# One ring for all bulk transfers, and one semaphore for all stores, in a layer-scale kernel

## The chip, the cores and the metric

The kernel runs on one core of a Trainium2 chip. The metric is device time in microseconds (us) of one execution. All runs named here were fast, at a granted clock of 1.0 (the share of its full clock that TensorE was given). A profile's span is some 1.3 us shorter than the time of the same execution (119.8 us against 121.17 us before the change), so spans are compared with spans and times with times.

Three words recur. A ring is the queue of transfers that one issuing engine (SP or ACT) fills. A packet is the piece of a transfer, here 32 KB, of which the trace has one record on a DMA engine. A transfer has landed when its semaphore says that all its data have arrived.

## The reference

```python
B, S, D = 1024, 16, 512            # x, y: bf16 (B, S, D); gamma: bf16 (D,)
def reference(x, y, gamma):
    return x + gamma * y
```

Two inputs of 16.8 MB are read and one output of 16.8 MB is written: 50.33 MB in all.

## The kernel before

Each of the 128 partitions gets 128 rows of 512 elements, in four pieces of 32 rows. A piece is 4 MB (4096 KB) of x, of y or of the output, and each partition's share of it is 32 KB in one run of memory. All of y has its place on the chip; x has two buffers that are used in turn, so the third x load must wait for the first addition, and the fourth for the second.

The x loads go through the SP ring, the y loads through the ACT ring, and the stores are shared between the two. VectorE multiplies y by gamma in place, then adds x in place.

```python
    # SP ring
    first.append(load(nc.sync, xs[0], xv[:, piece(0), :], s_x[0]))
    first.append(load(nc.sync, xs[1], xv[:, piece(1), :], s_x[1]))
    _take(s_sp, 1, nc.sync)                                   # first addition done
    load(nc.sync, xs[0], xv[:, piece(2), :], s_x[2])
    _take(s_sp, 1, nc.sync)                                   # second addition done
    load(nc.sync, xs[1], xv[:, piece(3), :], s_x[3])
    nc.sync.dma_start(out=ov[:, piece(0), :], in_=y_sb[:, piece(0), :]).then_inc(s_out_sp, 16)
    _take(s_sp, 1, nc.sync)
    nc.sync.dma_start(out=ov[:, piece(2), :], in_=y_sb[:, piece(2), :]).then_inc(s_out_sp, 16)
    # ACT ring (gamma was issued first)
    for c in range(n):
        i = load(nc.scalar, y_sb[:, piece(c), :], yv[:, piece(c), :], s_y[c])
        ...
    _take(s_act, 1, nc.scalar)
    nc.scalar.dma_start(out=ov[:, piece(1), :], in_=y_sb[:, piece(1), :]).then_inc(s_out_act, 16)
    _take(s_act, 1, nc.scalar)
    nc.scalar.dma_start(out=ov[:, piece(3), :], in_=y_sb[:, piece(3), :]).then_inc(s_out_act, 16)
    # VectorE, for each piece c
    ... tensor_tensor(out=yt, in0=yt, in1=gamma_sb broadcast, op=MULT)      # L98
    ... tensor_tensor(out=yt, in0=xs[c % 2], in1=yt, op=ADD)                # L104
    ...
    _take(s_out_sp, 32, nc.sync)                              # the end
    _take(s_out_act, 32, nc.sync)
```

Of the kernel before, what the change touches and what calls it, by code (L numbers as in the profile page):

```python
# [3 lines left out]

PIECE = 32
MULT, ADD = mybir.AluOpType.mult, mybir.AluOpType.add


def _take(sem, n, eng):


    return eng.wait_ge(sem, n).then_inc(sem, -n)  # L12


def kernel(
    tc: tile.TileContext,
    x: bass.AP,
    y: bass.AP,
    gamma: bass.AP,
    out: bass.AP,  # L20
):




    nc = tc.nc
    P = nc.NUM_PARTITIONS
    tc.close()
    tc.compile()  # L29

    xf = x.flatten_outer_dims()
    yf = y.flatten_outer_dims()
    of = out.flatten_outer_dims()
    N, D = xf.shape
    rows = N // P
    n = rows // PIECE
    dt = xf.dtype
    xv = xf.rearrange("(p n) d -> p n d", p=P)
    yv = yf.rearrange("(p n) d -> p n d", p=P)
    ov = of.rearrange("(p n) d -> p n d", p=P)  # L40

    gamma_row = nc.alloc_sbuf_tensor("gamma_row", [1, D], dt).ap()
    ones_row = nc.alloc_sbuf_tensor("ones_row", [1, P], dt).ap()
    gamma_sb = nc.alloc_sbuf_tensor("gamma_sb", [P, D], dt).ap()
    y_sb = nc.alloc_sbuf_tensor("y_sb", [P, rows, D], dt).ap()
    xs = [nc.alloc_sbuf_tensor(f"x{i}", [P, PIECE, D], dt).ap() for i in range(2)]
    gamma_ps = nc.alloc_psum_tensor("gamma_ps", [P, D], mybir.dt.float32).ap()

    sem = nc.alloc_semaphore
    s_gamma, s_ones, s_ps, s_dve = sem("s_gamma"), sem("s_ones"), sem("s_ps"), sem("s_dve")  # L50
    s_x = [sem(f"s_x{c}") for c in range(n)]
    s_y = [sem(f"s_y{c}") for c in range(n)]
    s_sp, s_act = sem("s_sp"), sem("s_act")
    s_out_sp, s_out_act = sem("s_out_sp"), sem("s_out_act")

    def piece(c):
        return slice(c * PIECE, (c + 1) * PIECE)

    first = []

    def load(eng, dst, src, s):
        return eng.dma_start(out=dst, in_=src).then_inc(s, 16)


    first.append(load(nc.scalar, gamma_row, gamma.unsqueeze(0), s_gamma))
    nc.vector.memset(ones_row, 1.0).then_inc(s_ones, 1)  # L66
    _take(s_ones, 1, nc.tensor)
    _take(s_gamma, 16, nc.tensor)
    nc.tensor.matmul(gamma_ps, ones_row, gamma_row, start=True, stop=True).then_inc(s_ps, 1)  # L69
    _take(s_ps, 1, nc.vector)  # L70
    nc.vector.tensor_copy(out=gamma_sb, in_=gamma_ps).then_inc(s_dve, 1)  # L71
    _take(s_dve, 1, nc.vector)


    first.append(load(nc.sync, xs[0], xv[:, piece(0), :], s_x[0]))
    first.append(load(nc.sync, xs[1], xv[:, piece(1), :], s_x[1]))
    _take(s_sp, 1, nc.sync)
    load(nc.sync, xs[0], xv[:, piece(2), :], s_x[2])
    _take(s_sp, 1, nc.sync)
    load(nc.sync, xs[1], xv[:, piece(3), :], s_x[3])  # L80
    nc.sync.dma_start(out=ov[:, piece(0), :], in_=y_sb[:, piece(0), :]).then_inc(s_out_sp, 16)
    _take(s_sp, 1, nc.sync)
    nc.sync.dma_start(out=ov[:, piece(2), :], in_=y_sb[:, piece(2), :]).then_inc(s_out_sp, 16)


    for c in range(n):
        i = load(nc.scalar, y_sb[:, piece(c), :], yv[:, piece(c), :], s_y[c])
        if c < 2:
            first.append(i)
    _take(s_act, 1, nc.scalar)  # L90
    nc.scalar.dma_start(out=ov[:, piece(1), :], in_=y_sb[:, piece(1), :]).then_inc(s_out_act, 16)
    _take(s_act, 1, nc.scalar)
    nc.scalar.dma_start(out=ov[:, piece(3), :], in_=y_sb[:, piece(3), :]).then_inc(s_out_act, 16)

    for c in range(n):
        yt = y_sb[:, piece(c), :]
        _take(s_y[c], 16, nc.vector)
        nc.vector.tensor_tensor(  # L98
            out=yt, in0=yt, in1=gamma_sb[:, None, :].to_broadcast([P, PIECE, D]), op=MULT
        ).then_inc(s_dve, 1)  # L100
        _take(s_x[c], 16, nc.vector)
        _take(s_dve, 1, nc.vector)

        i = nc.vector.tensor_tensor(out=yt, in0=xs[c % 2], in1=yt, op=ADD)  # L104
        if c == 0:
            i.then_inc(s_sp, 1)
        elif c == 1:
            i.then_inc(s_dve, 1)
            _take(s_dve, 1, nc.vector)
            nc.vector.sem_inc(s_sp, 1)  # L110
            nc.vector.sem_inc(s_act, 1)
        else:
            i.then_inc(s_sp if c == 2 else s_act, 1)

    _take(s_out_sp, 32, nc.sync)
    _take(s_out_act, 32, nc.sync)

    main = nc.main_func.blocks[0].instructions
    names = {i.ins.name for i in first}
    for b in nc.main_func.blocks[1:]:  # L120
        for i in [i for i in b.instructions if i.name in names]:
            b.instructions.remove(i)
    for k, i in enumerate(first):
        main.insert(1 + k, i.ins)


# [1 line left out]
_INS = ['x', 'y', 'gamma']  # L128
_OUTS = [((1024, 16, 512), 'bfloat16')]


# [23 lines left out]
```

## Time and profile before

| | before |
|---|---|
| time, median of the 3 runs | 121.11 us (121.06 to 121.39) |
| span of the profile | 119.8 us |
| VectorE busy | 70.3 us, done at 95.0 us |
| both DMA queues, share of the 16 engines' span | 49.9% + 48.7% = 98.6% |
| mean rate | 420 GB/s |

These lines are from the profile page of the kernel before. The rows with 40 digits or numbers are 40 slices of 3.0 us each; the lines q1 (the SP ring) and q10 (the ACT ring) give packets, MB, and the share of the 16 engines' span; the last two lines are the chain of work that ended last.

```profile
span 119.8 us, 90 instructions
PE 0.6 (0%) x1; PEld 0.1 (0%) x1; DVE 70.3 (59%) x10; POOL 0.2 (0%) x4
...
DMA  8999998989898989898999989999999999989994
GB/s 274 427 427 448 405 470 361 514 350 525 350 525 350 525 350 525 350 492 383 437 437 427 448 372 405 405 394 481 394 481 394 448 427 438 437 383 470 405 470 197
...
q1 hardware_dynamic: 864, 25.17, 49.9%
q10 hardware_dynamic: 866, 25.17, 48.7%
...
DVE 7%; issue 0%
DVE y_sb L104 7%
```

There is no idle slice in the DMA row, and the two shares add up to 98.6%. The chain at the bottom is of no use here: it follows instructions and stops at the last addition, since what came after it was only transfers. The alternation of 350 and 525 GB/s is not a real swing. A packet counts in the slice in which it starts, and a slice holds two or three packets of each engine.

These lines are from the timeline of the kernel before: start, duration, engine (SPq and ACTq are the issuing of DMAs), source line, operation.

```profile
24.24 8.69 DVE L98 TENSOR_TENSOR y_sb<-y_sb,gamma_sb 128x16384 bf16<-128x16384 bf16 x1 [18.12 <-DVEq L12]
...
59.56 0.35 ACTq L91 DMA_DIRECT2D out_dram<-y_sb  x1
...
86.31 8.69 DVE L104 TENSOR_TENSOR y_sb<-x,y_sb 128x16384 bf16<-128x16384 bf16 x1
95.11 0.35 ACTq L93 DMA_DIRECT2D out_dram<-y_sb  x1
```

VectorE stands still for 18 us at the start and ends 25 us before the span does. Neither costs anything as long as the DMA engines always have something to move.

The trace has a record of each DMA packet, and these give the sum of the span. All bulk data move in 1536 packets of 32 KB, 96 on each engine, and nearly every one takes 1.213 us. Over 16 engines that is 16 x 32768 bytes / 1.213 us = 432 GB/s. The Trainium skill ("DMA: Bandwidth & Descriptors", section "Where 436 GB/s comes from") puts the ceiling at 435.2 GB/s; this trace agrees within 1%. So 96 x 1.213 = 116.4 us of the span are fixed by the bytes, and only some 3 us are left to win or lose.

### The profile page before, as it was taken

What the parts mean: (1) busy time and instruction counts of PE and PEld (TensorE: products, weight loads), DVE (VectorE), ACT (ScalarE), POOL (GpSimd) and SP (SyncE); (2) the same over time, 40 slices, a digit from 0 to 9 for tenths busy, and PEclk for the clock granted to TensorE, in tenths of its full rate; (3) what the DMA queues carried; (4) which work ended last, traced back from release to release, by engine and by line L of the source; (5) the groups of instructions that cost most, each with busy time, mean ns of one, the idle gap of its engine ahead of it and who ended that gap; (6) DMA issues with size and microseconds to landing.
All of it is one profiled execution on the core that took longest, in us unless ns stands there. A gap on an engine that the chain in (4) does not pass through costs nothing. (4 is left out here: it accounts for less than half of the span.)

```text
span 119.8 us, 90 instructions
## 1 busy us (share of the span) xinstructions
PE 0.6 (0%) x1; PEld 0.1 (0%) x1; DVE 70.3 (59%) x10; POOL 0.2 (0%) x4
## 2 busy tenths in 40 slices
PE   0100000000000000000000000000000000000000
PEld 0000000000000000000000000000000000000000
DVE  0100000099999999999899999999999700000000
POOL 0000000000000000000000000000000000000000
DMA  8999998989898989898999989999999999989994
GB/s 274 427 427 448 405 470 361 514 350 525 350 525 350 525 350 525 350 492 383 437 437 427 448 372 405 405 394 481 394 481 394 448 427 438 437 383 470 405 470 197
DMA packets 1730, 50.33 MB, mean 420 GB/s; under 512 B 193, under 2 KB 194, under 8 KB 194
## 3 DMA queue, kind: packets, MB, share of 16 engines
q1 hardware_dynamic: 864, 25.17, 49.9%
q10 hardware_dynamic: 866, 25.17, 48.7%
HBM read 33.56 MB, written 16.78 MB: 420 GB/s over the span
## 5 line engine op out<-in xcount | busy, mean ns | idle before, releaser
L98 DVE TENSOR_TENSOR y_sb<-y_sb,gamma_sb 128x16384 bf16<-128x16384 bf16 x4 | 34.8, 8690 | 18.9 <-DVEq L12 18.9
L104 DVE TENSOR_TENSOR y_sb<-x,y_sb 128x16384 bf16<-128x16384 bf16 x4 | 34.8, 8692 | 0.6
L71 DVE CAST gamma_sb<-gamma_ps 128x512 bf16<-128x512 f32 x1 | 0.7, 692 | 2.6 <-DVEq L12 2.6
L66 DVE MEMSET ones_row<- 1x128 bf16 x1 | 0.2, 165 | 2.7 <-PEq L29 2.7
L69 PE MATMUL gamma_ps<-gamma_row,ones_row 1*128 1x512 bf16 x1 | 0.6, 581 | 4.7 <-PEq L12 4.7
L69 PEld LDWEIGHTS gamma_ps<-gamma_row,ones_row 1*128 1x128 bf16 x1 | 0.1, 98 | 4.7 <-issue 4.7
L139 POOL MEMSET const-bfloat16-1.0<- 128x1 bf16 x1 | 0.1, 101 | 0.0
L139 POOL MEMSET const-uint8-127<- 128x1 uint8 x1 | 0.1, 101 | 0.0
L139 POOL MEMSET const-float32-0.0<- 128x1 f32 x1 | 0.1, 98 | 0.2 <-issue 0.2
L139 POOL MEMSET const-float32-1.0<- 128x1 f32 x1 | 0.1, 98 | 0.0
## 6 DMA issues: line engine op xcount, KB each, us to landing
x<-in_x_dram SPq DMA_DIRECT2D x4, 4096.0 KB, 24.7
y_sb<-in_y_dram ACTq DMA_DIRECT2D x4, 4096.0 KB, 47.1
out_dram<-y_sb ACTq DMA_DIRECT2D x2, 4096.0 KB, 30.3
out_dram<-y_sb SPq DMA_DIRECT2D x2, 4096.0 KB, 42.1
gamma_row<-in_gamma_dram ACTq DMA_DIRECT2D x1, 1.0 KB
```

Source lines behind the costliest of these rows:

```text
L66: nc.vector.memset(ones_row, 1.0).then_inc(s_ones, 1)
L69: nc.tensor.matmul(gamma_ps, ones_row, gamma_row, start=True, stop=True).then_inc(s_ps, 1)
L71: nc.vector.tensor_copy(out=gamma_sb, in_=gamma_ps).then_inc(s_dve, 1)
L98: nc.vector.tensor_tensor(out=yt, in0=yt, in1=gamma_sb[:, None, :].to_broadcast([P, PIECE, D]), op=MULT).then_inc(s_dve, 1)
L104: i = nc.vector.tensor_tensor(out=yt, in0=xs[c % 2], in1=yt, op=ADD)
L139: nc = _bacc.Bacc("TRN2", target_bir_lowering=False, num_devices=1)
```

## The change

The intent: put every bulk load and store on the SP ring in one chosen order (all loads, then all stores), leave only the 1 KB load of gamma on the ACT ring, and count all stores on one semaphore that is waited for once, at the end. The diff, cut to its core:

```diff
+PIECES = [32, 32, 32, 32]
+X_AT = [0, 32, 0, 32]           # where each x piece lies in the buffer
+X_AFTER = [-1, -1, 0, 1]        # which addition frees it
+SP = [('x', 0), ('y', 0), ('x', 1), ('y', 1), ('y', 2), ('x', 2), ('y', 3), ('x', 3),
+      ('s', 0, 0, 0), ('s', 1, 1, 1), ('s', 2, 2, 2), ('s', 3, 3, 3)]
+ACT = [('g',)]
...
-    s_sp, s_act = sem("s_sp"), sem("s_act")
-    s_out_sp, s_out_act = sem("s_out_sp"), sem("s_out_act")
+    s_add, s_end, s_out = sem("s_add"), sem("s_end"), sem("s_out")
...
+            need = X_AFTER[args[0]] if kind == "x" else args[2] if kind == "s" else -1
+            if need > known:
+                eng.wait_ge(s_add, need + 1)
+                known = need
...
+                i = eng.dma_start(out=ov[:, r, :], in_=y_sb[:, r, :]).then_inc(s_out, 16)
+                stores += 1
...
+    ring(nc.sync, SP)
+    ring(nc.scalar, ACT)
...
-    _take(s_out_sp, 32, nc.sync)
-    _take(s_out_act, 32, nc.sync)
+    nc.scalar.sem_inc(s_end, 1)
+    _take(s_end, 1, nc.sync)
+    _take(s_add, n, nc.sync)
+    _take(s_out, 16 * stores, nc.sync)
```

The arithmetic of VectorE is unchanged. Not shown in the cut: the issues moved to the front of the program are now x0, y0 and gamma, where they were x0, x1, y0, y1 and gamma.

More of the change, by code (lines that the diff above doesn't have):

```diff
@@ L3 @@
 from concourse import mybir
-PIECE = 32
+PIECES = [32, 32, 32, 32]
+X_AT = [0, 32, 0, 32]
+X_AFTER = [-1, -1, 0, 1]
+SP = [('x', 0), ('y', 0), ('x', 1), ('y', 1), ('y', 2), ('x', 2), ('y', 3), ('x', 3), ('s', 0, 0, 0), ('s', 1, 1, 1), ('s', 2, 2, 2), ('s', 3, 3, 3)]
+ACT = [('g',)]
+EARLY = [('x', 0), ('y', 0), ('g',)]
 MULT, ADD = mybir.AluOpType.mult, mybir.AluOpType.add
@@ L35 @@
     rows = N // P
-    n = rows // PIECE
+    n = len(PIECES)
+    assert sum(PIECES) == rows
+    starts = [sum(PIECES[:c]) for c in range(n + 1)]
     dt = xf.dtype
@@ L45 @@
     y_sb = nc.alloc_sbuf_tensor("y_sb", [P, rows, D], dt).ap()
-    xs = [nc.alloc_sbuf_tensor(f"x{i}", [P, PIECE, D], dt).ap() for i in range(2)]
+    x_rows = max(a + r for a, r in zip(X_AT, PIECES))
+    x_sb = nc.alloc_sbuf_tensor("x_sb", [P, x_rows, D], dt).ap()
     gamma_ps = nc.alloc_psum_tensor("gamma_ps", [P, D], mybir.dt.float32).ap()
@@ L52, with piece, x_tile, ring @@
     s_y = [sem(f"s_y{c}") for c in range(n)]
-    s_sp, s_act = sem("s_sp"), sem("s_act")
-    s_out_sp, s_out_act = sem("s_out_sp"), sem("s_out_act")
-    def piece(c):
-        return slice(c * PIECE, (c + 1) * PIECE)
-    first = []
-    def load(eng, dst, src, s):
-        return eng.dma_start(out=dst, in_=src).then_inc(s, 16)
-    first.append(load(nc.scalar, gamma_row, gamma.unsqueeze(0), s_gamma))
+    s_add, s_end, s_out = sem("s_add"), sem("s_end"), sem("s_out")
+    def piece(a, b=None):
+        return slice(starts[a], starts[(a if b is None else b) + 1])
+    def x_tile(c):
+        return x_sb[:, X_AT[c] : X_AT[c] + PIECES[c], :]
+    early, stores = [], 0
+    def ring(eng, what, known=-1):
+        nonlocal stores
+        for w in what:
+            kind, args = w[0], w[1:]
+            need = X_AFTER[args[0]] if kind == "x" else args[2] if kind == "s" else -1
+            if need > known:
+                eng.wait_ge(s_add, need + 1)
+                known = need
+            if kind == "g":
+                i = eng.dma_start(out=gamma_row, in_=gamma.unsqueeze(0)).then_inc(s_gamma, 16)
+            elif kind == "x":
+                c = args[0]
+                i = eng.dma_start(out=x_tile(c), in_=xv[:, piece(c), :]).then_inc(s_x[c], 16)
+            elif kind == "y":
+                c = args[0]
+                i = eng.dma_start(out=y_sb[:, piece(c), :], in_=yv[:, piece(c), :])
+                i.then_inc(s_y[c], 16)
+            else:
+                r = piece(args[0], args[1])
+                i = eng.dma_start(out=ov[:, r, :], in_=y_sb[:, r, :]).then_inc(s_out, 16)
+                stores += 1
+            if w in EARLY:
+                early.append(i.ins)
+    ring(nc.sync, SP)
+    ring(nc.scalar, ACT)
     nc.vector.memset(ones_row, 1.0).then_inc(s_ones, 1)
@@ L72 @@
     _take(s_dve, 1, nc.vector)
-    first.append(load(nc.sync, xs[0], xv[:, piece(0), :], s_x[0]))
-    first.append(load(nc.sync, xs[1], xv[:, piece(1), :], s_x[1]))
-    _take(s_sp, 1, nc.sync)
-    load(nc.sync, xs[0], xv[:, piece(2), :], s_x[2])
-    _take(s_sp, 1, nc.sync)
-    load(nc.sync, xs[1], xv[:, piece(3), :], s_x[3])
-    nc.sync.dma_start(out=ov[:, piece(0), :], in_=y_sb[:, piece(0), :]).then_inc(s_out_sp, 16)
-    _take(s_sp, 1, nc.sync)
-    nc.sync.dma_start(out=ov[:, piece(2), :], in_=y_sb[:, piece(2), :]).then_inc(s_out_sp, 16)
-    for c in range(n):
-        i = load(nc.scalar, y_sb[:, piece(c), :], yv[:, piece(c), :], s_y[c])
-        if c < 2:
-            first.append(i)
-    _take(s_act, 1, nc.scalar)
-    nc.scalar.dma_start(out=ov[:, piece(1), :], in_=y_sb[:, piece(1), :]).then_inc(s_out_act, 16)
-    _take(s_act, 1, nc.scalar)
-    nc.scalar.dma_start(out=ov[:, piece(3), :], in_=y_sb[:, piece(3), :]).then_inc(s_out_act, 16)
     for c in range(n):
@@ L98 @@
         nc.vector.tensor_tensor(
-            out=yt, in0=yt, in1=gamma_sb[:, None, :].to_broadcast([P, PIECE, D]), op=MULT
+            out=yt, in0=yt, in1=gamma_sb[:, None, :].to_broadcast([P, PIECES[c], D]), op=MULT
         ).then_inc(s_dve, 1)
@@ L102 @@
         _take(s_dve, 1, nc.vector)
-        i = nc.vector.tensor_tensor(out=yt, in0=xs[c % 2], in1=yt, op=ADD)
-        if c == 0:
-            i.then_inc(s_sp, 1)
-        elif c == 1:
-            i.then_inc(s_dve, 1)
-            _take(s_dve, 1, nc.vector)
-            nc.vector.sem_inc(s_sp, 1)
-            nc.vector.sem_inc(s_act, 1)
-        else:
-            i.then_inc(s_sp if c == 2 else s_act, 1)
-    _take(s_out_sp, 32, nc.sync)
-    _take(s_out_act, 32, nc.sync)
+        nc.vector.tensor_tensor(out=yt, in0=x_tile(c), in1=yt, op=ADD).then_inc(s_add, 1)
+    nc.scalar.sem_inc(s_end, 1)
+    _take(s_end, 1, nc.sync)
+    _take(s_add, n, nc.sync)
+    _take(s_out, 16 * stores, nc.sync)
     main = nc.main_func.blocks[0].instructions
-    names = {i.ins.name for i in first}
+    names = {i.name for i in early}
     for b in nc.main_func.blocks[1:]:
@@ L122 @@
             b.instructions.remove(i)
-    for k, i in enumerate(first):
-        main.insert(1 + k, i.ins)
+    for k, i in enumerate(early):
+        main.insert(1 + k, i)
 _INS = ['x', 'y', 'gamma']
```

## The prediction

> **What bounds the kernel now.** The 16 DMA engines. The page shows VectorE busy 70.3 of 119.8 us and the DMA row at 8 to 9 tenths in every slice but the last; the two queues fill 49.9% and 48.7% of the engines' span, moving 50.33 MB at a mean of 420 GB/s. The chain that ended last names only one 8.69 us addition (7%), since it cannot see transfers. VectorE waits 18.1 us at the start and is done at 95.0 us, 25 us before the end.
>
> The packet records of the trace give the sum: 1536 packets of 32 KB, 96 per engine, nearly all of 1.213 us; 96 x 1.213 = 116.4 us. The first starts at 1.0 us. The rest: first packets of about 1.8 us (0.65 us extra per engine); a slow patch from 73 to 77 us, where load packets of the SP ring took 1.3 to 2.4 us just as the ACT ring went from its last load to its first store (0.88 us per engine, more on the slowest); engines that end unevenly, 118.6 to 119.4 us; some 0.35 us from the last packet to its landing.
>
> **What the change removes, adds, moves.** Bytes, packets and the eight 8.69 us VectorE passes stay. Two alternating rings become one. The Trainium skill ("DMA: Bandwidth & Descriptors", "Issuing engines are not separate DMA queues") says that DMAs of different issuing engines run on the same 16 engines and interleave. The trace agrees: from 38.7 to 42 us only the ACT ring had packets, back to back at 1.213 us, across a border of two transfers too. So one ring should cost nothing.
>
> Does it run dry? At an estimated 9.7 us per 4 MB transfer (8 packets x 1.213), x0 lands at about 11 us, y0 at 21, y1 at 40, x2 at 60, x3 at 79. Additions end at about 38, 57.5, 75 and 93 us. The third x load must wait for the first addition (38) while the ring has work until 50; the fourth for the second (57.5) with work until 69; the last store for the fourth (93) with work until 108. Margins of 11 us or more: no starvation. VectorE starts at about 21 us instead of 24.2, off the critical path.
>
> Loads are no longer mixed with stores (before: 75 to 85 us), but mixed packets took 1.213 us too: no gain. One switch from loads to stores remains; I expect a slow patch of 0.3 to 1 us at about 79 us. One end wait fewer is worth 0.07 us; engines ending more evenly, up to 0.4 us.
>
> **Prediction.** 120.7 us, 8 in 10 between 119.9 and 121.5. The floor is a span of about 118.5 us, some 119.8 us as timed (timed runs are 1.3 us above the span), so faster by 2% (118.7) is nearly excluded: 0.01. Within 2%: 0.97. Slower by over 2%: 0.02.
>
> **What the profile would show.** Right: almost all bytes on one queue, 98 to 99% of the span; the first multiplication at about 21 us; stores from near 79 us, back to back, a short dip in GB/s there. Wrong: a gap in the DMA row at about 50, 69 or 108 us (starvation), or packets longer than 1.213 us throughout (one ring being slower).
>
> **What would make it wrong.** A limit on what one ring can queue, so that issuing stalls; idle time at transfer borders that the second ring covered; no slow patch (about 119.8), or a larger one.

## The result, and the profile after

| | before | after |
|---|---|---|
| time, median (lowest to highest) of 4 runs each | 121.16 us (121.06 to 121.39) | 121.02 us (120.77 to 121.06) |
| ratio, after over before | | 0.9981, 95% interval 0.9961 to 1.0001 |
| span of the profile | 119.8 us | 119.7 us |

A ratio here is the mean time of one kernel's fast runs over that of the other's of the same rounds, so it is not quite the ratio of the medians quoted.

The same lines of the page of the changed kernel:

```profile
span 119.7 us, 84 instructions
PE 0.6 (0%) x1; PEld 0.1 (0%) x1; DVE 70.2 (59%) x10; POOL 0.2 (0%) x4
...
DMA  7989898989898999999898989999999999999894
GB/s 241 460 372 504 372 504 350 525 350 525 350 514 361 482 394 438 438 427 449 383 493 372 504 350 525 350 350 482 394 438 438 405 471 394 471 394 482 372 504 186
...
q1 hardware_dynamic: 1728, 50.33, 98.5%
q10 hardware_dynamic: 2, 0.00, 0.1%
...
DVE 7%; issue 0%
DVE y_sb L120 7%
```

Everything went from q10 to q1, and the sum of the shares stayed (98.6%, and 98.5% + 0.1%). The one visible mark is in the GB/s row. Numbers of 350 and about 500 alternate, but the 26th and 27th (from 74.8 to 80.8 us) are both 350: this is the switch from loads to stores.

From the timeline of the changed kernel (L115 is the multiplication, L120 the addition, L88 the x load, L95 the stores):

```profile
21.96 8.69 DVE L115 TENSOR_TENSOR y_sb<-y_sb,gamma_sb 128x16384 bf16<-128x16384 bf16 x1 [18.08 <-DVEq L22]
...
39.52 0.33 SPq L88 DMA_DIRECT2D x_sb<-in_x_dram  x1
...
58.94 0.33 SPq L88 DMA_DIRECT2D x_sb<-in_x_dram  x1
59.31 34.85 SPq L95 DMA_DIRECT2D out_dram<-y_sb  x4
...
85.10 8.69 DVE L120 TENSOR_TENSOR y_sb<-x_sb,y_sb 128x16384 bf16<-128x16384 bf16 x1
```

VectorE starts 2.3 us earlier (21.96 against 24.24) and ends 1.2 us earlier, and nobody profits. The waits of the SP ring's issuing, in the changed kernel (who waited for whom: us in total, times, longest):

```profile
SPq L88 <- DVE y_sb L120: 54.9, 2, 36.3
SPq L95 <- DVE y_sb L120: 33.2, 2, 17.1
SPq L22 <- SPq L22: 25.4, 1, 25.4
```

The issuing of the only ring now stands still for VectorE for 88 us, and still the engines never run out. When the third x load is issued at 39.5 us, the ring has loads until y2 has landed at 51.0 us; when the fourth is issued at 58.9 us, it has loads until y3 has landed at 70.4 us. A long wait of the issuing is harmless as long as it ends before the work already queued does.

The packet records of both kernels, summed. "Longer than 1.213" is the sum over all 32 KB packets of what each took beyond 1.213 us, divided by 16 engines.

```text
us                                      before   after
first bulk packet starts                  1.01    1.01
96 packets x 1.213                      116.45  116.45
longer than 1.213, first 5 us             0.65    0.62
longer than 1.213, after that             0.96    0.81
last packet ends, earliest engine       118.61  118.51
last packet ends, latest engine         119.38  119.35
last store landed                       119.74  119.70
end of span                             119.84  119.74
```

Only the earliest engine starts at 1.01 us; the mean over the engines is 1.12 us before and 1.24 us after (one engine started at 2.01 us). With these means the first four lines add up to 119.17 and 119.12 us, some 0.26 us more than the mean of the engines' last ends (118.91 and 118.85 us), because the records of neighbouring packets mostly overlap by 4 ns.

### The profile page after: what moved, and what is told of

Read it like the earlier page. It is cut to its first block, busy times and chain, and to the rows that moved or that the text cites. A ratio compares the mean times of both kernels' runs of the same rounds, so it can differ in the third digit from the quotient of the medians.

```text
span 119.7 us, 84 instructions
## 1 busy us (share of the span) xinstructions
PE 0.6 (0%) x1; PEld 0.1 (0%) x1; DVE 70.2 (59%) x10; POOL 0.2 (0%) x4
## 3 DMA queue, kind: packets, MB, share of 16 engines
q1 hardware_dynamic: 1728, 50.33, 98.5%
## 5 line engine op out<-in xcount | busy, mean ns | idle before, releaser
L115 DVE TENSOR_TENSOR y_sb<-y_sb,gamma_sb 128x16384 bf16<-128x16384 bf16 x4 | 34.8, 8688 | 20.0 <-DVEq L22 20.0
L120 DVE TENSOR_TENSOR y_sb<-x_sb,y_sb 128x16384 bf16<-128x16384 bf16 x4 | 34.8, 8692 | 0.6
```

The costliest lines, as they stand in the source:

```text
L115: nc.vector.tensor_tensor(out=yt, in0=yt, in1=gamma_sb[:, None, :].to_broadcast([P, PIECES[c], D]), op=MULT).then_inc(s_dve, 1)
L120: nc.vector.tensor_tensor(out=yt, in0=x_tile(c), in1=yt, op=ADD).then_inc(s_add, 1)
```

## The experiments

All are edits of the changed kernel. Each was timed beside fresh runs of the kernel before on the same chip: 11 runs in each of the three batches, with medians of 121.18 us (the first four experiments), 121.24 us (the next three) and 121.17 us (the last three). The changed kernel was not run again in these batches, so a difference from its 121.02 us goes across batches and chips, and one of 0.1 us is not read as an effect.

### Is one ring worth something, against two?

```diff
-SP = [x0, y0, x1, y1, y2, x2, y3, x3, s0, s1, s2, s3]     # list shortened here
-ACT = [('g',)]
+SP = [x0, x1, x2, x3, s0, s1, s2, s3]
+ACT = [('g',), ('y', 0), ('y', 1), ('y', 2), ('y', 3)]
```

> The changed kernel with its four y loads moved to the ACT ring, the rest (waits, store order, one semaphore for the stores) left. Theory A (the 16 DMA engines' packet time decides; rings only interleave): within 0.2 us of the changed kernel, 120.8 to 121.2 us, packets of 1.213 us throughout, one slow patch before the first store. Rival B (one ring against two is worth something by itself, and a loss elsewhere in the change hides it): over 0.5 us away from 121.0 us, in either direction.

Measured: 120.90 us (6 runs, 120.80 to 120.97), ratio to before 0.9975 (0.9962 to 0.9988). It is 0.12 us from the changed kernel, inside what theory A expected; rival B falls. From its page, the same bytes on two queues:

```profile
q1 hardware_dynamic: 1152, 33.55, 66.2%
q10 hardware_dynamic: 578, 16.78, 32.6%
```

The Trainium skill ("DMA: Bandwidth & Descriptors", section "Issuing engines are not separate DMA queues") says that DMAs of different issuing engines run on the same engines and interleave, and that using several saves only issuing time. This pair of runs agrees.

### Is one semaphore for the stores worth something?

```diff
 ... (four semaphores s_outs, one for each store)
-    _take(s_out, 16 * stores, nc.sync)
+    for s in s_outs:
+        _take(s, 16, nc.sync)                 # one semaphore for each store
```

> The changed kernel with one semaphore for each store, waited for one after the other at the end. Theory A: the first three have landed by 110 us, so each of their waits costs about 0.07 us or nothing, before the last landing; same as the changed kernel within 0.1 us (121.0 us), the last landing at about 119.7 us of the span. Rival C (the way the end is waited for is worth time): 0.2 us or more slower.

Measured: 120.96 us (6 runs, 120.86 to 121.22), ratio to before 0.9984 (0.9968 to 0.9999). In the trace the first three waits are over at 94.3, 100.2 and 109.9 us, and only the fourth is there at the end. The last store landed at 119.55 us and the span ended at 119.59 us. Rival C falls: what counts is that no wait is left after the last landing, and not how many there are.

### Does VectorE matter?

This kernel gives a wrong result: the multiplication is left out.

```diff
-        nc.vector.tensor_tensor(out=yt, in0=yt, in1=gamma_sb[...], op=MULT).then_inc(s_dve, 1)
-        _take(s_dve, 1, nc.vector)
```

> Wrong result on purpose: out = x + y, the four multiplications (34.8 us of VectorE) left out. Theory A (DMA bound): 121.0 us plus or minus 0.3, VectorE busy about 35 us. Rival D (VectorE's passes or its waits decide): 5 us or more faster.

Measured: 121.03 us (4 runs, 120.90 to 121.23). From its page:

```profile
PE 0.6 (0%) x1; PEld 0.1 (0%) x1; DVE 35.6 (30%) x6; POOL 0.2 (0%) x4
...
q1 hardware_dynamic: 1728, 50.33, 98.8%
```

Half of VectorE's work was gone (35.6 us busy instead of 70.2) and the time did not move by 0.1 us. Rival D falls.

### Do the bytes matter?

Also wrong: the last store is left out of the list.

```diff
-      ('s', 0, 0, 0), ('s', 1, 1, 1), ('s', 2, 2, 2), ('s', 3, 3, 3)]
+      ('s', 0, 0, 0), ('s', 1, 1, 1), ('s', 2, 2, 2)]
```

> Wrong result on purpose: the last of the four stores is left out (eight packets fewer per engine). Theory A: 8 x 1.213 = 9.7 us less, 111.3 us plus or minus 0.3. Rival D: less than 5 us faster, since all computing stays.

Measured: 111.32 us (4 runs, 111.08 to 111.62), ratio 0.9186. From its page:

```profile
span 109.8 us, 83 instructions
PE 0.6 (1%) x1; PEld 0.1 (0%) x1; DVE 70.2 (64%) x10; POOL 0.2 (0%) x4
...
q1 hardware_dynamic: 1584, 46.14, 98.5%
```

All computing stayed, and the time fell by 121.02 - 111.32 = 9.70 us, where 8 x 1.213 = 9.70 us was expected. That it agrees to the hundredth is luck: the four runs spread over 0.5 us, and the spans of the two profiles differ by 10.0 us. This and the run above show the bound from both sides: half of VectorE's work costs no time here, and a packet costs about its 1.213 us.

### What does the order cost if the ring does run dry?

The second piece's store is moved ahead of three loads that could have gone first.

```diff
-SP = [x0, y0, x1, y1, y2, x2, y3, x3, s0, s1, s2, s3]     # lists shortened here
+SP = [x0, y0, x1, y1, y2, s1, x2, y3, x3, s0, s2, s3]
```

> The second piece's store is put right behind the third y load, so that the ring waits for the second addition (ends about 59 us) with work only until about 51 us; all loads behind it wait too. Theory A: the engines stand idle for 9 to 10 us from about 51 us[...], and nothing gives it back: 130 to 131.5 us. Rival E (later slack absorbs it, since VectorE ends 25 us before the end): under 125 us.

Measured: 131.69 us (4 runs, 131.46 to 131.96), ratio 1.0865; the median is 0.2 us above the expected range. From its page, and from a table of windows (busy time of each engine in each stretch of 10 us, then the clock, the DMA share and GB/s):

```profile
DMA  9799899989989973007998999899899999999995
...
q1 hardware_dynamic: 1728, 50.33, 91.4%
```

```profile
core 0: us, PE busy (x) PEld busy (x) DVE busy (x) POOL busy (x), PEclk, DMA share, GB/s
40.00:50.00 10.00, 0.00 (x0) 0.00 (x0) 8.67 (x1) 0.00 (x0) 1.00 0.97 419
50.00:60.00 10.00, 0.00 (x0) 0.00 (x0) 9.85 (x3) 0.00 (x0) 1.00 0.12 52
60.00:70.00 10.00, 0.00 (x0) 0.00 (x0) 7.46 (x1) 0.00 (x0) 1.00 0.94 367
```

The last load packet ended at 50.39 us, the store was issued at 58.89 us when the second addition was done, and its first packet started at 59.74 us, 0.84 us after the issue. That is 9.3 to 9.8 us without a packet on every engine, 9.6 us in the mean. Nothing gave it back, although VectorE in the changed kernel ends 26 us before the span does; rival E falls. Long packets add 1.1 us: 1.79 us per engine here, 0.72 us in the changed kernel (only those of over 1.25 us counted, without the start). Together this is the 10.5 us by which the span is longer, within 0.2 us. So one ring does have a price, and this kernel avoids it by its order alone. A wait on a shared ring holds up everything behind it.

### The slow patch at the switch from loads to stores

In both kernels some packets were long around the first store: 1.3 to 2.4 us from 73 to 77 us before, up to 2.0 us from 76.7 to 80 us after. Five runs asked when that happens: the two below with a store moved forward, the first of them once more, and the two further down without computing.

```diff
 # early_store
+SP = [x0, y0, x1, y1, y2, s0, x2, y3, x3, s1, s2, s3]
 # tiny_store: row 0 of 32 early, rows 1 to 31 at the end
+SP = [x0, y0, x1, y1, y2, s0[0:1], x2, y3, x3, s0[1:32], s1, s2, s3]
```

> The first piece's store is moved between the third y load and the third x load; no wait runs the ring dry. Question: the slow patch of 0.7 us per engine before the first store (76.7 to 80 us in the changed kernel). Theory F (it comes with the first store only): one patch, now at about 48 to 52 us, none at about 88 us; 121.0 us plus or minus 0.2. Rival G (every switch from loads to stores costs it): two patches, at about 49 and 88 us, 121.6 to 121.9 us. Rival H (it has to do with the time or with the addresses of the last loads, not with stores): a patch still at about 75 to 80 us or in the last x load, none at 49 us.

> One row of 32 of the first piece's store (128 packets of 1 KB) is moved between the third y load and the third x load; the other 31 rows stay at the end. Theory F (the first store pays, whatever its size): a patch at about 49 to 51 us and none at 77 to 80 us; 121.0 us plus or minus 0.2. Rival G (a switch of bulk transfer pays): the patch stays at 77 to 80 us, near its 0.7 us per engine.

Measured: early_store 121.45 us (6 runs, 121.32 to 121.63), ratio 1.0018 (1.0004 to 1.0032); tiny_store 120.86 us (6 runs, 120.67 to 121.00), ratio 0.9968 (0.9954 to 0.9982). In early_store the patch was at 48 us and there was next to none at 88 us (0.01 us per engine), which contradicts rivals G and H; but the time rose by 0.4 us where theory F expected none, and load packets from 33 to 48 us were slightly long too. In tiny_store the patch stayed at 77 to 80 us: a first store of 1 KB packets does not use it up. So theory F as written falls, and what remains is "the first bulk store".

> The kernel of early_store once more, unchanged. In its first profile the load packets from 33 to 48 us took 1.25 to 1.35 us, before the program differs from the changed kernel in what the engines do, and it was 0.4 us slower in all its runs. If that was a chance of that placement: packets of 1.213 us there and 121.0 us now. If it belongs to the program: again 121.4 us and the long packets.

Measured: 121.29 us (6 runs, 121.16 to 121.37), ratio 1.0007 (0.9994 to 1.0020). The long packets from 33 to 47 us were gone, so the program does not bring them with it; but the time was again 0.3 us above the changed kernel's, and the patch was again early, and this time larger (1.10 us per engine at 47 to 50 us).

Then the computing was taken away altogether (out = y, wrong), so that the order could be chosen freely. Each store waits for the landing of its y.

```diff
-        (both tensor_tensor calls and their waits)
-                eng.wait_ge(s_add, need + 1)
+                eng.wait_ge(s_x[need] if kind == "x" else s_y[need], 16)
 # copy_one_switch keeps the order; copy_three_switches:
+SP = [x0, y0, x1, s0, y1, x2, s1, y2, y3, x3, s2, s3]
```

> Wrong result on purpose: no multiplication and no addition at all (out = y); the ring has the changed kernel's order, each store waits for the landing of its y instead of an addition, each late x load for the landing of the earlier x. Theory A (the engines' packets decide, computing does not): 121.0 us plus or minus 0.3 with VectorE nearly idle, and a slow patch of about 0.7 us per engine at 77 to 80 us still. If the patch came from VectorE's passes beside the transfers: no patch, 120.2 us.

> The same without computing, but the order goes from loads to stores three times (about 31, 60 and 99 us) and back twice (about 41 and 70 us), with the ring never dry. Theory F (only the first store after loads pays the patch): one patch near 30 us, time as copy_one_switch within 0.2 us. Rival G (every switch from loads to stores pays about 0.7 us): three patches, 1.4 us slower than copy_one_switch. The earlier runs contradict each other here: one patch in two switches with one store early, but two patches when the ring had run dry.

Measured: copy_one_switch 120.91 us (5 runs, 120.89 to 121.10), ratio 0.9980; copy_three_switches 121.73 us (6 runs, 121.39 to 121.84), ratio 1.0039. From the page of copy_one_switch:

```profile
PE 0.6 (0%) x1; PEld 0.1 (0%) x1; DVE 0.9 (1%) x2; POOL 0.2 (0%) x4
...
q1 hardware_dynamic: 1728, 50.33, 98.8%
```

With VectorE all but idle (0.9 us) the time is the changed kernel's, and the patch is there as well (0.53 us per engine at 77 us). The patch is thus not made by VectorE's passes. The packet records of all these runs (us per engine beyond 1.213 us, in packets of over 1.25 us, after the start; "first store" is when its first packet began):

```text
kernel               first store   long packets, at (us)
before                   76.3      0.85, at 73 to 76
after                    79.8      0.72, at 76 to 80
two_rings                78.8      0.65, at 76 to 79
tiny_store    50.2 (tiny), 80.1    0.06 at 47 to 49; then 0.63, at 77 to 80
copy_one_switch          80.1      0.53, at 77 to 78
early_store              51.3      0.58, at 48 to 49, and 0.55 spread over 33 to 48
early_store_2            51.1      1.10, at 47 to 50
copy_three_switches      31.7      1.05, at 28 to 31; then 0.07 at 59 to 61, 0.07 at 97 to 100
dry_ring                 59.7      0.83, at 68 to 69; then 0.87 at 96 to 100
```

One thing is the same in all these traces but dry_ring's: the long packets are loads, and nearly all of the patch lies in the last two packets of each engine before the first bulk store (in the kernel before, in the SP ring's loads just before the ACT ring's first store). The store's own first packets took their usual time, 1.213 us, but for one of 1.31 us in two_rings.

In copy_three_switches only the first of three switches costs much; the other two cost 0.07 us each. That speaks for "the first bulk store, once". But dry_ring does not fit: there the first store began without a patch after the idle time, its last packets were long, and the next switch was long as well. What the patch is stays open. What is shown: it costs 0.5 to 1.1 us, it occurs in every kernel tried (twice in dry_ring), and it needs no computing. Its size is not steady: two profiles of one program, early_store and early_store_2, had 0.58 and 1.10 us, and those of the changed kernel's order 0.53 to 0.89 us (four_sems 0.57, no_multiply 0.89). So whether an early bulk store makes it larger is not shown, though early_store was 0.3 to 0.4 us slower than the changed kernel in both its batches. copy_three_switches was 0.8 us slower than copy_one_switch in the medians, of which the two profiles show only 0.3; the profiled execution was the fastest of the one and the slowest of the other.

None of these versions, if right in its result, beats both kernels by anything that matters: the best, tiny_store and two_rings, are 0.12 to 0.16 us below the changed kernel's median.

## Why the prediction was right

- **The bound: right.** The engines' packet time decides. Half of VectorE's work left out changed nothing; eight packets per engine left out gave 9.70 us, as computed; and all computing left out changed nothing.
- **One ring costs nothing: right.** 98.5% on one queue, packets of 1.213 us; two rings with the same waits and the same order of stores are within 0.12 us.
- **No starvation: right, with the margins about as said.** The additions ended at 39.5, 58.9, 76.4 and 93.8 us instead of 38, 57.5, 75 and 93, but the landings were late too: the three margins were 11.5, 11.5 and 16.2 us instead of 12, 11.5 and 15. The estimate of the landings left out the slow first packets (0.6 us) and the time from the last packet to the landing (0.35 us), so x0 landed at 12.1 us and y0 at 21.8 us. The dry ring showed what a negative margin would have cost.
- **The slow patch: right in size (0.72 us; 0.3 to 1 was predicted) and nearly in place** (76.7 to 80 us; about 79 was predicted). It was carried over from the trace of the kernel before and not explained, and its size varies from profile to profile, so a part of this is luck.
- **One end wait fewer: right.** From the last landing to the end it took 0.03 us instead of 0.10 us. Before, the SP ring's stores landed last (119.74 us) and were waited for first, so the wait for the ACT ring's (landed at 118.53 us) came after them. four_sems, with four waits in the order of landing, also has 0.03 us.
- **The one term that failed: "engines ending more evenly, up to 0.4 us".** The engines' last packets ended between 118.51 and 119.35 us after the change (0.84 us apart) and between 118.61 and 119.38 us before (0.77 us apart): nothing was gained. This is probably most of why the time was 121.02 us, 0.3 us above the point predicted and inside its range; the prediction does not say how its point was summed.

The range, 119.9 to 121.5 us, held the time before (121.16 us) too, so "nothing changes" would have met it as well. What tests the mechanism is the experiments, and not that the number fell inside.

Whether the remaining 0.14 us between the medians is real, the runs of the change alone do not settle (the interval reaches 1.0001). two_rings, four_sems, tiny_store and copy_one_switch, which all send the bulk of the loads before the stores, have ratios of 0.9968 to 0.9984 with intervals below 1, on two rings and on one, with one semaphore and with four (no_multiply, of the same order, has 0.9988, and its interval reaches 1.0005). So a gain of about 0.2% to 0.3%, 0.2 to 0.4 us, is likely. Of it 0.07 us is the end: every one of these kernels has 0.03 us from the last landing to the end, where the kernel before has 0.10 us. The rest could belong to the order of loads and stores, but the slow patch alone varies by more than that from profile to profile; this is not isolated.

## What to carry to other kernels

Before moving transfers between rings, add up the DMA packets: if packets per engine times the time of one packet already make 97% of the span (116.4 of 119.8 us here), no assignment to rings and no way of waiting can give more than the rest. One ring was then as good as two here (within 0.12 us), and simpler, but its order has to be checked: list when each wait on it ends and until when the work already queued will last. Where a wait ended later than that, everything behind it was late by the difference and the start of the new transfer (0.84 us), and slack on the compute engine did not give it back (10.7 us in dry_ring).

## What the Trainium skill lacked or had wrong

- "DMA: Bandwidth & Descriptors", "Where 436 GB/s comes from", says that for transfers between HBM and SBUF the HBM side, about 358 GB/s, binds. Here one core alone kept 432 GB/s in steady state, loads and stores alike. "HBM Reference", "Specifications (TRN2)", has it right: a core that streams alone is bounded by its 16 DMA engines.
- No page has the slow patch: in the last two load packets of each engine before the first bulk store, packets of 1.213 us took up to 2.4 us, 0.5 to 1.1 us per engine in all, once in most kernels. Its cause is open.
- No page says that the first bulk packet of each engine is longer: 1.63 to 1.98 us before and 1.60 to 2.21 us after instead of 1.213 us, some 0.6 us per engine at the start. One engine after the change was the exception: it began 1 us later and took 1.23 us.
- "DMA: Bandwidth & Descriptors", "Latency and other measured facts", gives about 600 ns to the first byte on this path and does not say from where it counts. To the first packet's start it was 0.84 us when the ring was dry (58.89 to 59.74 us) and 1.0 us at the kernel's start, counted from the start of the issuing instruction; counted from its end, 0.49 and 0.63 us, which is near the page. When the other ring kept the engines busy it was far longer: the third x load of the kernel before was issued at 41.87 us, and its first packet started at 45.39 us, 3.5 us later (the same in two_rings).
